# A reordered opening and other limits by stretch, in a kernel of four attention layers

## The chip, the cores and the metric

The kernel runs on one NeuronCore of one Trainium2 chip. The metric is the device time of one execution in microseconds (us), the median over runs. The engines named below are TensorE (PE, its weight loads PEld), VectorE (DVE), ScalarE (ACT), GpSimd (POOL) and the queue of SyncE (SP), which issues nearly all DMAs.

## The reference

The input `x` has 2048 tokens of 512 features, in bf16. Four layers run over it, A, B, A, B, each with a residual:

```python
x = x + _A_ref(_layernorm(x), A_wq, A_wk, A_wv, A_wo, A_beta)
x = x + _B_ref(_layernorm(x), B_wqkv, B_wo)
x = x + _A_ref(_layernorm(x), A_wq, A_wk, A_wv, A_wo, A_beta)
x = x + _B_ref(_layernorm(x), B_wqkv, B_wo)
```

Layer A cuts the tokens into 4 segments of 512. Each of 32 heads (16 wide) does causal softmax attention within the segment. Beside it stands a linear memory: with phi(t) = t + 1 for positive t and exp(t) otherwise, the sums M of phi(k) v and z of phi(k) over earlier segments give phi(q) M / (phi(q) z + 1e-6). A gate, the sigmoid of `beta` per head, mixes the two, and `wo` projects the mix. Layer B is plain attention over all 2048 tokens with 32 heads, so every query meets every key. Exponentials therefore dominate: each head of a B layer has 2048 x 2048 of them.

## The kernel before, in words

Nothing is looped on the chip. A Python planner writes one list of instructions for each engine, and semaphores follow from the reads and writes that each instruction declares. The planner estimates when each engine will be done (class Sched, `estimate`) and decides by these estimates what comes next; each engine then executes its list in order.

The attention is cut into units. One unit holds up to 3 banks of PSUM, a bank being 128 keys by 512 queries of one head. TensorE multiplies 32 rows of keys with masked queries `qm`, so that 4 heads share a row group (lines 545, 1577); ScalarE takes the exponential of the unit's banks in one instruction (line 1687) into `pT`; two units later TensorE multiplies `pT` with the values and a column of ones. The masked queries come from multiplying the queries `QA` or `QB` with a column of `par`, which is 1 for every second head's 16 features. In layer A the causal mask is either added by TensorE or applied by POOL (line 1701).

Some banks don't go through ScalarE. For them VectorE computes the exponential in integer arithmetic from PSUM: a first pass (line 1209, `dx_first`) and two adds (line 1263), into spare tiles (`dxt`, and parts of KA, QA, VA, wA, wB when these are free). A unit is then 2 banks for ScalarE and up to 2 for VectorE.

Projections, normalizations, the memory of layer A and the output projections are background tasks (Python generators). After each unit the planner runs as many of their steps as its credits and estimates allow. All thresholds of these decisions are class attributes. `PLAN` overrides some of them for a stretch of 40 units, by number; `set_limits` installs a stretch's row when its first unit comes.

The opening goes this way. SP issues the loads of the first four tiles of `x`, then the weights wk, wq, wv of layer A, `beta`, the rest of `x`, and the other weights. POOL builds the identity, the masks and constants. VectorE sums the head mask into `par` (line 667). TensorE runs `WARM` = 84 products of the identity with itself (line 651, `warm_up`), so that its clock is up. VectorE takes the statistics of the first four tiles (lines 711, 713), ScalarE their square root (719), and then loads its table for exponentials with an exponential of a constant (720). VectorE inverts (721) and normalizes the four tiles (752, into xn and oT). TensorE transposes them (580); ScalarE and VectorE copy the two halves out to `xT` (766, 767). Behind the transposes `WARM2` = 20 more products run. Then the projections of the first chunk of 128 features follow (`proj_fm`): keys, then queries, 4 products each, copied out by VectorE and ScalarE in turn (605, 603). With both the first unit can start.

Of the kernel before, what the change touches and what calls it, by code (L numbers as in the profile page):

```python
# [7 lines left out]
ALU = mybir.AluOpType  # L8
# [320 lines left out]
class Builder:  # L329
# [22 lines left out]
        20: dict(DX_LATE=900, EVAC_ACT=300, SLACK=550, PV_SKIP=500, BACK=6, CR_B=1200, R_PAIRS=2, MASK_PE=800, DIV_LATE=2500, BUSY_WAIT=500, GAP=1, BG_BANK=100, QWAIT=3, QMIN=3, HOLD_AT=40, LN1_AT=6, BUSY_BACK=800),  # L352
        21: dict(FILL_DVE=200, BACK=6, FILL=0.53, CR_W=1300, CR_B=1800, CR_A=1700, CARRY_W=0, NEARW=20, LEVEL=3, BG_BANK=400, QMIN=1, HOLD_MAX=0),
        22: dict(ACT1=200, DX_LATE=500, NEAR=10, PV_SKIP=200, EARLY=500, CR_B=1800, CARRY_W=1500, OPART=2, DX_LAG=3, MASK_PE=800, LEVEL=3, DIV_LATE=2500, DVE_LATE=800, BG_BANK=100, QUAD=0, LN1_AT=6),
        23: dict(R_LATE=1200, R_NEAR=50, FILL_DVE=200, BACK=8, CR_A=1200, NEARW=40, OPART=4, PAIRS=999, LEVEL=3, TAKEN=0.25, QUAD=0, QMIN=4, HOLD_SEGS=2),
        24: dict(R_LATE=1500, DX_LATE=900, EVAC_ACT=100, REST=12, NEAR=8, TAKEN_A=1, R_NEAR=50, PV_SKIP=100, EARLY=500, FILL_DVE=200, CR_W=1300, CR_A=1200, DX_LAG=1, LOW=20, POOL_QM=1),
        25: dict(ACT1=300, MARGIN=600, R_LATE=2200, EVAC_ACT=1500, NEAR=18, CR_W=1900, CR_B=1800, R_PAIRS=2, DX_LAG=1, PAIRS=999, DIV_LATE=800, TAKEN=0.25, DVE_LATE=800, BG_BANK=400, PHI_LATE=300),
        26: dict(MARGIN=800, REST=10, SLACK=350, EARLY=500, FILL_DVE=200, BUSY_ROOM=300, BACK=8, CR_W=1500, R_PAIRS=2, PAIRS=24, DIV_LATE=800, TAKEN=0.3, BG_BANK=100, QWAIT=8, QMIN=4, LN1_AT=6),
        27: dict(MARGIN=800, REST=4, SLACK=350, EARLY=500, FILL_DVE=200, BUSY_ROOM=300, BACK=8, CR_W=1500, PART=1, R_PAIRS=2, PAIRS=999, DIV_LATE=800, TAKEN=0.3, BG_BANK=100, QWAIT=8, QMIN=4, LN1_AT=6),
        28: dict(MARGIN=800, NEAR=5, SLACK=350, R_NEAR=10, CARRY_W=400, OPART=3, PAIRS=60, DIV_LATE=2500, TAKEN=0.3, DVE_LATE=800, BUSY_BACK=800),  # L360
        29: dict(DX_BANK=900, SLACK=700, PV_SKIP=100, EARLY=100, BUSY_ROOM=300, FILL=0.47, CR_W=1500, PART=3, R_PAIRS=2, TAKEN=0.3, DVE_LATE=800, LN1_AT=3, BUSY_BACK=800),
        30: dict(ACT1=900, MARGIN=800, REST=12, SLACK=700, PV_SKIP=100, EARLY=100, FILL=0.42, CR_W=1500, CARRY_W=400, PART=3, R_PAIRS=2, MASK_PE=800, DIV_LATE=2500, DVE_LATE=800, QWAIT=3),
        31: dict(DX_LATE=900, DX_BANK=700, REST=20, PV_SKIP=100, BUSY_ROOM=900, FILL=0.57, CR_A=1700, PART=3, R_PAIRS=2, OPART=4, MASK_PE=800, TAKEN=0.3, DVE_LATE=800, BG_BANK=100, QWAIT=3, QMIN=4),
        32: dict(MARGIN=400, DX_LATE=900, NEAR=12, PV_SKIP=100, FILL_DVE=100, BUSY_ROOM=300, FILL=0.55, CR_W=1500, R_PAIRS=2, TAKEN=0.3, GAP=3, DVE_LATE=800, QWAIT=8, QMIN=1, HOLD_AT=40),
        33: dict(MARGIN=350, DX_LATE=900, EVAC_ACT=800, NEAR=12, R_NEAR=20, PV_SKIP=100, EARLY=500, FILL=0.5, CR_W=1500, R_PAIRS=2, TAKEN=0.3, DVE_LATE=800, QWAIT=8, BUSY_BACK=800),
        34: dict(ACT1=900, R_LATE=2200, NEAR=18, BACK=2, FILL=0.55, CR_W=1500, R_PAIRS=2, DX_LAG=3, TAKEN=0.3, PE_LOW=4, GAP=3, DVE_LATE=800, QMIN=3),
        35: dict(DX_LATE=900, DX_BANK=700, REST=20, PV_SKIP=100, BUSY_ROOM=900, FILL=0.57, CR_A=1700, PART=3, R_PAIRS=2, OPART=4, MASK_PE=800, TAKEN=0.3, DVE_LATE=800, BG_BANK=400, QWAIT=3, QMIN=4),
        36: dict(ACT1=900, R_LATE=2200, REST=16, PV_SKIP=900, BUSY_ROOM=300, FILL=0.51, CR_B=1200, R_PAIRS=2, NEARW=90, OPART=4, DIV_LATE=800, DVE_LATE=800, QWAIT=8, QMIN=4, HOLD_MAX=1),
        37: dict(R_LATE=2200, DX_LATE=900, DX_BANK=900, NEAR=18, CR_W=1900, CR_B=1800, PAIRS=24, DIV_LATE=800, PE_LOW=7, DVE_LATE=800, QUAD=0),
        38: dict(REST=8, SLACK=250, R_NEAR=20, CR_W=1300, R_PAIRS=2, NEARW=90, LEVEL=1, TAKEN=0.3, LOW=20, DVE_LATE=800, QUAD=0),  # L370
# [255 lines left out]
    def setup(self):  # L626
# [24 lines left out]
        self.warm_up(self.WARM)  # L651
# [13 lines left out]
        for e_ in range(2):  # L665
            hv = hm[:, :].rearrange("p (r two) -> p two r", two=2)[:, e_, :]
            self.op("dve", (lambda e_, hv: lambda e: e.tensor_reduce(self.par[:, e_:e_ + 1], hv, axis=mybir.AxisListType.X,
                                                                     op=ALU.add))(e_, hv),
                    reads=[self.b_hm], writes=[self.b_par])
# [8 lines left out]
    def warm_up(self, n):  # L678

        al = self.new_alloc()  # L680
        for _ in range(n):
            self.mm(self.ps[:, 2560:2560 + P], self.ident[:, :], self.ident[:, :], True, True, [self.b_ident], self.banks[5], al, n=P)
# [20 lines left out]
    def ln_part(self, L, s):  # L703
# [14 lines left out]
        if (L, s) == (0, 0):  # L718
            self.op("act", lambda e: e.activation(v, var, ACT.Sqrt, bias=self.eps[:, 0:1]), reads=self.b_lnst[k] + [self.b_eps], writes=[bw], ns=230)
            self.op("act", lambda e: e.activation(self.eps[:, 1:2], self.eps[:, 0:1], ACT.Exp), reads=[self.b_eps], writes=[self.b_eps], ns=1500)  # L720
            self.op("dve", lambda e: e.reciprocal(y, v), reads=[bw], writes=[bw], ns=165)
            return k
# [22 lines left out]
    def ln_first(self, k, slot):  # L745
# [9 lines left out]
        for j in range(2):  # L755
            bank, al = self.misc(), self.new_alloc()
            base = bank.idx * 1024
            for i, (xn, bx) in enumerate(xns[2 * j:2 * j + 2]):
                for c in range(NCH):
                    o = base + c * 256 + i * 128  # L760
                    self.tr(self.psb[:, o:o + 128], xn[:, c * 128:(c + 1) * 128], [bx], bank, al)
            if j:
                self.warm_up(self.WARM2)
            src = self.psb[:, base:base + 1024].rearrange("p (c j) -> p c j", c=NCH)
            dst = self.xT[:, slot, :, j * 256:(j + 1) * 256]
            eng, fn = (("act", lambda dst, src: lambda e: e.activation(dst, src, ACT.Copy)),
                       ("dve", lambda dst, src: lambda e: e.tensor_copy(dst, src)))[j]
            self.op(eng, fn(dst, src), writes=self.b_xT[slot][2 * j:2 * j + 2], bank=bank, alloc=al, ns=(1023, 690)[j])
# [51 lines left out]
    def task_A(self, L, s):  # L820
# [1268 lines left out]
```

## Time and profile before

| | |
|---|---|
| time, median of 3 runs | 1742.31 us (1740.94 to 1742.91) |
| profiled execution, its time | 1744.39 us |
| profiled execution, its span | 1742.7 us |
| ScalarE busy | 1701.9 us (98%) |
| TensorE busy | 1627.4 us (93%) |
| VectorE busy | 1521.1 us (87%) |
| GpSimd busy | 211.6 us (12%) |
| exponentials of line 1687 | 1548 instructions, 1669.7 us |

Busy time is the time in which an engine executes instructions, without its waits. The span runs from the first to the last instruction. A row of the timeline gives start, duration, engine, line, operation, what is written and read, and in brackets the idle time ahead of it and what ended it. A row that merges several instructions lasts from the first one's start to the last one's end. A product on TensorE is pipelined: its duration covers its way through the array, and the next one starts earlier than it ends.

### The profile page before, as it was taken

The page shows a single profiled execution, that of the slowest core. Times are in us where ns is not written, and L with a number is a line of the kernel's source. Part 1 is how long each engine was busy: PE and PEld are TensorE (multiplying, and loading weights), DVE is VectorE, ACT ScalarE, POOL GpSimd, SP SyncE. Part 2 cuts the span into 40 slices and gives each one's busy share as a digit, 9 for nine tenths or more (in the row PEclk, how much of TensorE's full clock was granted, in tenths as well). Part 3 has the DMA queues.
Part 4 walks back from the last instruction along what each step waited for, and adds up shares of the span by engine and source line. Part 5 has one row for each costly group of instructions (what it writes and reads, how often), then busy time and mean ns, then how long its engine had stood idle before and what let it go on. Part 6 is the DMA issues. An engine that isn't in the chain of part 4 may idle for free.

```text
span 1742.7 us, 46922 instructions
## 1 busy us (share of the span) xinstructions
PE 1627.4 (93%) x19534; PEld 580.4 (33%) x19534; DVE 1521.1 (87%) x2937; ACT 1701.9 (98%) x1594; POOL 211.6 (12%) x325
## 2 busy tenths in 40 slices
PE   8899899999999999999999999999999999999999
PEld 5553434322222523522225222432222222222226
DVE  6757576999998699899996999989999999999997
ACT  7899999999999999999999999999999999999998
POOL 2211301110200402100003010210021000000000
PEclk9999999999999999999999999999999999999999
DMA  6110211000212131102111202011011100000000
GB/s 176 35 24 19 38 20 26 14 14 8 32 22 59 29 92 35 30 9 59 47 19 32 56 14 56 16 25 44 8 26 26 22 11 17 20 11 17 16 14 18
DMA packets 148439, 54.56 MB, mean 31 GB/s; under 512 B 128769, under 2 KB 147713, under 8 KB 148225
## 3 DMA queue, kind: packets, MB, share of 16 engines
q1 hardware_dynamic: 148224, 51.56, 13.8%
q8 instruction: 153, 2.51, 0.6%
q14 instruction: 62, 0.50, 0.1%
HBM read 18.88 MB, written 2.10 MB: 12 GB/s over the span
## 4 chain that ended last, share of the span: by engine, by line
ACT 46%; PE 30%; issue 13%; DVE 9%; DMA 1%; SPq 1%; POOL 0%; ACTq 0%; DVEq 0%; POOLq 0%
ACT pT L1687 45%; PE ps L545 30%; DVE KA L1209 1%; DVE wA L1209 1%; DVE dxt L1209 1%; DMA tb<-ub 1%; DVE wB L1209 1%; ACT amem L806 1%; SPq L612 0%; DVE lnst L711 0%; DVE qm L1577 0%; DVE dxt L1263 0%; DVE ub L1813 0%; DVE wB L1280 0%; DVE wA L1263 0%
## 5 line engine op out<-in xcount | busy, mean ns | idle before, releaser
L1687 ACT ACTIVATE pT<-ps 128x1024 bf16<-128x1024 f32 (+1 forms) x1548 | 1669.7, 1247 | 25.1 <-PE ps L545 20.2
L545 PE MATMUL ps<-qm,KB 32*128 32x512 bf16 x4096 | 561.3, 385 | 80.8 <-ACT pT L1687 65.5
L545 PE MATMUL ps<-pT,VB 128*17 128x512 bf16 x2912 | 496.2, 384 | 1.1 <-DVE wB L1209 0.3
L545 PEld LDWEIGHTS ps<-qm,KB 32*128 32x128 bf16 x4096 | 145.3, 91 | 608.7 <-ACT pT L1687 512.6
L1209 DVE TENSOR_SCALAR KA<-ps 128x512 uint16<-128x512 f32 (+1 forms) x412 | 298.1, 730 | 15.2 <-PE ps L545 11.5
L1209 DVE TENSOR_SCALAR dxt<-ps 128x512 uint16<-128x512 f32 (+1 forms) x320 | 232.1, 729 | 18.6 <-PE ps L545 15.7
L545 PE MATMUL ps<-dxt,VB 128*17 128x512 bf16 x987 | 215.9, 382 | 0.0
L545 PEld LDWEIGHTS ps<-pT,VB 128*17 128x17 bf16 x2912 | 115.8, 87 | 286.3 <-issue 273.3
L1834 POOL TENSOR_TENSOR ob<-tb,rd 128x512 bf16<-128x512 bf16 x31 | 34.5, 1114 | 806.2 <-DVE rd L1830 791.0
L545 PE MATMUL ps<-QA,VB 128*17 128x512 bf16 x423 | 124.3, 381 | 0.0
L1701 POOL TENSOR_SCALAR_AFFINE_SELECT pT<-pT 128x512 bf16<-128x512 bf16 (+4 forms) x132 | 70.1, 545 | 416.1 <-ACT pT L1687 416.1
L1209 DVE TENSOR_SCALAR wA<-ps 128x512 uint16<-128x512 f32 (+1 forms) x166 | 117.8, 716 | 2.3 <-PE ps L545 1.0
L545 PE MATMUL ps<-VA,VB 128*17 128x512 bf16 x423 | 116.8, 381 | 0.0
L545 PE MATMUL ps<-woB,zero 128*32 128x512 bf16 (+1 forms) x346 | 113.4, 383 | 0.1
L545 PE MATMUL ps<-wA,VB 128*17 128x512 bf16 x528 | 111.6, 382 | 0.0
L545 PE MATMUL ps<-qm,KA 32*128 32x128 bf16 (+2 forms) x1536 | 93.5, 256 | 18.5 <-ACT pT L1687 13.2
L545 PE MATMUL ps<-KA,VB 128*17 128x512 bf16 x423 | 107.3, 381 | 0.0
L545 PE MATMUL ps<-VA,pT 128*128 128x51 bf16 (+1 forms) x2540 | 103.9, 188 | 2.0 <-POOL pT L1701 0.9
L1577 POOL TENSOR_SCALAR qm<-QB,par 128x512 bf16<-128x512 bf16 x98 | 76.2, 788 | 232.3 <-PE ps L545 213.3
L1263 DVE TENSOR_SCALAR dxt<-dxt 128x1024 uint16<-128x1024 uint16 (+1 forms) x238 | 95.6, 425 | 1.3
L545 PEld LDWEIGHTS ps<-VA,pT 128*128 128x128 bf16 x2540 | 89.2, 97 | 20.7 <-issue 6.0
L1209 DVE TENSOR_SCALAR wB<-ps 128x512 uint16<-128x512 f32 (+1 forms) x110 | 85.1, 781 | 1.8 <-PE ps L545 0.8
(167 smaller groups left out, 1947.2 us busy)
## 6 DMA issues: line engine op xcount, KB each, us to landing
wB<-in_B_wqkv_dram SPq DMA_DIRECT2D x48, 128.0 KB, 2.4
wA<-in_A_wk_dram SPq DMA_DIRECT2D x16, 128.0 KB, 2.3
wA<-in_A_wq_dram SPq DMA_DIRECT2D x16, 128.0 KB, 2.4
wA<-in_A_wv_dram SPq DMA_DIRECT2D x16, 128.0 KB, 2.5
out_dram<-x SPq DMA_DIRECT2D x8, 256.0 KB, 2.2
x<-in_A_x_dram SPq DMA_DIRECT2D x3, 512.0 KB, 8.5
wB<-in_B_wqkv_dram SPq DMA_DIRECT2D x1, 1536.0 KB, 11.8
oT<-ob SPq DMA_TRANSPOSE x63, 2.5
```

The source lines that it names most:

```text
L545: self.sc.add("pe", lambda e: e.matmul(out, lhsT, rhs, start=start, stop=stop, skip_group_check=True), reads=reads, banks=[(bank, "w", all ...
L806: self.op("act", lambda e: e.activation(et, src, ACT.Exp), reads=bsrc, writes=self.b_amem, ns=1023, gap=915)
L1209: self.op("dve", lambda e: e.tensor_scalar(d, o, SCALE * LOG2E * 128, 127.0 * 128 + EXP_BIAS, op0=ALU.mult, op1=ALU.add), writes=[self.b_d ...
L1263: self.op("dve", (lambda d, s, c: lambda e: e.tensor_scalar(d, s, float(c), None, op0=ALU.add))(d, s, c), reads=[self.b_dxt[b][0]], writes ...
L1577: self.op(eng, (lambda m, q, col: lambda e: e.tensor_scalar(m, q, col, 0.0, op0=ALU.mult, op1=ALU.add))(m, q, col), reads=[bq, self.b_par] ...
L1687: self.sc.add("act", (lambda dst, src: lambda e: e.activation(dst, src, ACT.Exp, scale=SCALE))(dst, src), writes=self.b_pT[slot * 3 + i:sl ...
L1701: self.op("pool", (lambda blk, pat: lambda e: e.affine_select(blk, blk, pattern=pat, compare_op=ALU.is_ge, fill=0.0, base=0, channel_multi ...
L1834: self.op(eng, lambda e: e.tensor_tensor(ob, t[:, :, :, 0:16], rb, ALU.mult), reads=[br] + self.b_tb, writes=self.b_ob[oi], **(dict(ns=125 ...
```

## The change

Four things change.

- `par`, the two sums over the head mask, is no longer computed in the setup but in a new method `parity`, called behind the square root of the first statistics.
- `warm_up` takes a width. The 84 products ahead of the first transposes have 78 columns instead of 128, the 20 behind them 96.
- In the first chunk of the first segment of the first layer, queries are projected ahead of keys. The two take turns at being copied out by VectorE and ScalarE as before, so VectorE now copies the queries and ScalarE the keys.
- In `PLAN`, 18 of the rows 20 to 38 have other values (row 23 is as before). Rows 0 to 19 and 39 stay.

```diff
-        20: dict(DX_LATE=900, EVAC_ACT=300, SLACK=550, PV_SKIP=500, BACK=6, CR_B=1200, R_PAIRS=2, MASK_PE=800, DIV_LATE=2500, BUSY_WAIT=500, GAP=1, BG_BANK=100, QWAIT=3, QMIN=3, HOLD_AT=40, LN1_AT=6, BUSY_BACK=800),
+        20: dict(MARGIN=600, DX_LATE=900, EVAC_ACT=300, SLACK=550, PV_SKIP=100, CR_B=1200, R_PAIRS=2, MASK_PE=800, DIV_LATE=2500, BUSY_WAIT=500, GAP=1, BG_BANK=100, QWAIT=3, QMIN=3, HOLD_AT=40, LN1_AT=6, BUSY_BACK=800),
...
-        34: dict(ACT1=900, R_LATE=2200, NEAR=18, BACK=2, FILL=0.55, CR_W=1500, R_PAIRS=2, DX_LAG=3, TAKEN=0.3, PE_LOW=4, GAP=3, DVE_LATE=800, QMIN=3),
+        34: dict(MARGIN=350, DX_LATE=900, EVAC_ACT=800, NEAR=12, R_NEAR=20, PV_SKIP=100, EARLY=500, FILL=0.5, CR_W=1500, CARRY_W=0, R_PAIRS=2, DX_LAG=1, TAKEN=0.3, LOW=30, DVE_LATE=800, HOLD_SEGS=2, BUSY_BACK=800),
...
@@ setup
-        self.warm_up(self.WARM)
+        self.warm_up(self.WARM, 78)
...
-        for e_ in range(2):
-            hv = hm[:, :].rearrange("p (r two) -> p two r", two=2)[:, e_, :]
-            self.op("dve", (lambda e_, hv: lambda e: e.tensor_reduce(self.par[:, e_:e_ + 1], hv, axis=mybir.AxisListType.X,
-                                                                     op=ALU.add))(e_, hv),
-                    reads=[self.b_hm], writes=[self.b_par])
...
+    def parity(self):
+
+        for e_ in range(2):
+            hv = self.hmask[:, :].rearrange("p (r two) -> p two r", two=2)[:, e_, :]
+            self.op("dve", (lambda e_, hv: lambda e: e.tensor_reduce(self.par[:, e_:e_ + 1], hv, axis=mybir.AxisListType.X,
+                                                                     op=ALU.add))(e_, hv),
+                    reads=[self.b_hm], writes=[self.b_par])
+
+    def warm_up(self, n, w):
 
         al = self.new_alloc()
         for _ in range(n):
-            self.mm(self.ps[:, 2560:2560 + P], self.ident[:, :], self.ident[:, :], True, True, [self.b_ident], self.banks[5], al, n=P)
+            self.mm(self.ps[:, 2560:2560 + w], self.ident[:, :], self.ident[:, 0:w], True, True, [self.b_ident], self.banks[5], al, n=w)
...
@@ ln_part, first segment of the first layer
             self.op("act", lambda e: e.activation(self.eps[:, 1:2], self.eps[:, 0:1], ACT.Exp), reads=[self.b_eps], writes=[self.b_eps], ns=1500)
+            self.parity()
             self.op("dve", lambda e: e.reciprocal(y, v), reads=[bw], writes=[bw], ns=165)
...
@@ ln_first
-                self.warm_up(self.WARM2)
+                self.warm_up(self.WARM2, 96)
...
@@ task_A
         for c in range(NCH):
-            yield from self.proj_fm(self.wA, self.b_wA[1], 512, slot, c, self.KA[:, sl, c, :], self.b_KA[sl][c])
-            self.flags.add(("K", L, s, c))
-            yield from self.proj_fm(self.wA, self.b_wA[0], 0, slot, c, self.QA[:, sl, c, :], self.b_QA[sl][c])
-            self.flags.add(("Q", L, s, c))
+            pair = [("K", 1, self.KA, self.b_KA), ("Q", 0, self.QA, self.b_QA)]
+            for nm, i, dst, bd in pair[::-1] if (L, s, c) == (0, 0, 0) else pair:
+                yield from self.proj_fm(self.wA, self.b_wA[i], 512 * i, slot, c, dst[:, sl, c, :], bd[sl][c])
+                self.flags.add((nm, L, s, c))
```

More of the change, by code (lines that the diff above doesn't have):

```diff
@@ L355 @@
+        22: dict(ACT1=200, DX_LATE=500, NEAR=10, PV_SKIP=200, EARLY=500, FILL=0.53, CR_B=1800, CARRY_W=1500, OPART=2, DX_LAG=1, MASK_PE=800, LEVEL=3, DIV_LATE=800, DVE_LATE=800, BG_BANK=100, QUAD=0, LN1_AT=6),
         23: dict(R_LATE=1200, R_NEAR=50, FILL_DVE=200, BACK=8, CR_A=1200, NEARW=40, OPART=4, PAIRS=999, LEVEL=3, TAKEN=0.25, QUAD=0, QMIN=4, HOLD_SEGS=2),
-        24: dict(R_LATE=1500, DX_LATE=900, EVAC_ACT=100, REST=12, NEAR=8, TAKEN_A=1, R_NEAR=50, PV_SKIP=100, EARLY=500, FILL_DVE=200, CR_W=1300, CR_A=1200, DX_LAG=1, LOW=20, POOL_QM=1),
@@ L369 @@
-        37: dict(R_LATE=2200, DX_LATE=900, DX_BANK=900, NEAR=18, CR_W=1900, CR_B=1800, PAIRS=24, DIV_LATE=800, PE_LOW=7, DVE_LATE=800, QUAD=0),
-        38: dict(REST=8, SLACK=250, R_NEAR=20, CR_W=1300, R_PAIRS=2, NEARW=90, LEVEL=1, TAKEN=0.3, LOW=20, DVE_LATE=800, QUAD=0),
+        24: dict(R_LATE=1500, DX_LATE=900, EVAC_ACT=100, REST=12, NEAR=8, TAKEN_A=1, SLACK=250, R_NEAR=50, PV_SKIP=100, EARLY=500, FILL_DVE=200, CR_W=1300, CR_A=1200, DX_LAG=1, LOW=20, BG_BANK=100, POOL_QM=1),
+        25: dict(ACT1=300, MARGIN=600, R_LATE=2200, EVAC_ACT=1500, NEAR=18, CR_W=1900, CR_B=1800, R_PAIRS=2, DX_LAG=1, PAIRS=999, DIV_LATE=800, TAKEN=0.5, DVE_LATE=800, BG_BANK=400, PHI_LATE=300),
@@ L371 @@
+        38: dict(DX_LATE=700, REST=8, SLACK=250, R_NEAR=20, CR_W=1300, R_PAIRS=2, NEARW=90, PAIRS=999, LEVEL=1, LOW=20, GAP=1, DVE_LATE=800, BG_BANK=400, QUAD=0),
         39: dict(R_LATE=2200, CR_W=1900, R_PAIRS=2, PAIRS=24, DIV_LATE=800),
```

26 lines of the change are left out of this document (12 added, 14 removed).

## The prediction

> **What bounds the kernel now.** I read the page's first part, then the windows cut at every 40th exponential of line 1687 (the planner changes its limits there), then the timeline of the opening.
>
> ```profile
> PE 1627.4 (93%) x19534; PEld 580.4 (33%) x19534; DVE 1521.1 (87%) x2937; ACT 1701.9 (98%) x1594; POOL 211.6 (12%) x325
> ```
> ```profile
> 973.70:1191.60 217.90, 207.11 (x2459) 71.95 (x2458) 199.28 (x410) 216.46 (x204) 22.93 (x42) 1.00 0.15 37
> 1191.60:1705.40 513.80, 482.99 (x5028) 130.81 (x5023) 506.55 (x825) 512.88 (x522) 41.10 (x44) 1.00 0.08 16
> 1705.40:1742.70 37.30, 33.06 (x741) 22.38 (x737) 24.69 (x55) 30.12 (x32) 0.00 (x0) 0.98 0.05 17
> 14.20:82.80 68.60, 61.57 (x932) 33.26 (x932) 50.15 (x142) 60.22 (x52) 21.92 (x43) 1.00 0.31 78
> 82.80:254.40 171.60, 156.30 (x2039) 68.79 (x2039) 107.95 (x229) 163.05 (x129) 28.33 (x42) 0.97 0.16 27
> 254.40:973.70 719.30, 674.64 (x8230) 242.91 (x8222) 625.56 (x1260) 712.08 (x655) 94.44 (x140) 1.00 0.16 33
> ```
>
> The columns are stretch, length, then busy time of PE, PEld, DVE, ACT, POOL. ScalarE is the bound: of 1742.7 us it idles 40.8, and in the stretches whose limits change (20 to 38, from 973.7 us) only 1.4 + 0.9 + 7.2. There a bank of exponentials can leave ScalarE only by going to VectorE, which idles 18.6 us in the first of these windows and 7.3 in the second, which is full. The first exponential waits until 14.2 us, and what is saved ahead of it moves everything behind it:
>
> ```profile
> 1.43 7.54 PE L545 MATMUL ps<-ident 128*128 128x128 bf16 x84 [1.43 <-POOL eps L650]
> ...
> 2.75 0.35 DVE L667 TENSOR_REDUCE par<-hmask 128x1 f32<-128x4 f32 x2 [2.75 <-POOL hmask L660]
> 3.01 0.68 DVE L711 BATCH_NORM_STATS2 lnst<-x 128x6 f32<-128x512 bf16 x1
> 3.15 0.51 SPq L635 DMA_DIRECT2D wA<-in_A_wq_dram  x1
> ...
> 6.11 0.18 DVE L713 BATCH_NORM_AGGREGATE lnst<-lnst 128x2 f32<-128x6 f32 x1
> 6.33 0.30 ACT L719 ACTIVATE lnw<-lnst,eps 128x4 f32<-128x4 f32 x1 [1.73 <-DVE lnst L713]
> ...
> 6.66 0.18 DVE L721 RECIPROCAL lnw<-lnw 128x4 f32<-128x4 f32 x1 [0.37 <-ACT lnw L719]
> 6.87 0.74 DVE L752 TENSOR_SCALAR xn<-x,lnst,lnw 128x512 bf16<-128x512 bf16 x2
> 7.53 0.73 DVE L752 TENSOR_SCALAR oT<-x,lnst,lnw 128x512 bf16<-128x512 bf16 x2
> 7.94 0.20 ACT L720 ACTIVATE eps<-eps 128x1 f32<-128x1 f32 x1
> ...
> 8.81 0.61 PE L580 MATMUL ps<-ident,xn 128*128 128x128 bf16 x8
> ...
> 9.25 0.61 PE L580 MATMUL ps<-ident,oT 128*128 128x128 bf16 x8
> 9.45 1.02 ACT L766 ACTIVATE xT<-ps 128x1024 bf16<-128x1024 bf16 x1 [1.31 <-PE ps L580]
> ...
> 9.70 1.28 PE L545 MATMUL ps<-ident 128*128 128x128 bf16 x20
> 9.90 0.69 DVE L767 COPY xT<-ps 128x1024 bf16<-128x1024 bf16 x1 [1.64 <-PE ps L580]
> ...
> 10.82 1.89 PE L545 MATMUL ps<-xT,wA 128*128 128x512 bf16 x8
> ...
> 11.88 0.69 DVE L605 CAST KA<-ps 128x512 bf16<-128x512 f32 x1 [1.29 <-PE ps L545]
> 12.74 0.60 ACT L603 ACTIVATE QA<-ps 128x512 bf16<-128x512 f32 x1 [2.27 <-PE ps L545]
> 13.37 0.61 DVE L1577 TENSOR_SCALAR qm<-QA,par 128x512 bf16<-128x512 bf16 x2 [0.80 <-ACT QA L603]
> ...
> 13.78 0.39 PE L545 MATMUL ps<-qm,KA 32*128 32x512 bf16 x3 [1.08 <-DVE qm L1577]
> ...
> 14.22 2.79 ACT L1687 ACTIVATE pT<-ps 128x1536 bf16<-128x1536 f32 x2 [0.88 <-PE ps L545]
> ```
>
> Start, duration, engine and line. The first normalized tile is done at 6.87 + 0.41 = 7.28 us (two take 0.74, overlapping a little), but its transposes start at 8.81, because 84 warming products stand ahead of them on TensorE. Behind the transposes 20 more run to 10.8, while the two copies of xT end at 10.47 and 10.59. Then keys go through VectorE, queries through ScalarE, and the masked queries (1577) come last, with the product at 13.78.
>
> **The change, part by part.** The pace of a narrow product comes from these rows:
>
> ```profile
> 1.43 5.73 PE L545 MATMUL ps<-ident 128*128 128x128 bf16 x52 [1.43 <-POOL eps L650]
> ```
> ```profile
> 31.89 0.78 PE L545 MATMUL ps<-VA,pT 128*128 128x34 bf16 x24
> ```
> ```profile
> L545 PE MATMUL ps<-ident x104: 219/288/311, 1.4 to 10.8; 128*128 128x128 bf16 x104
> ```
>
> *84 products of 78 columns.* 52 products start within 5.73 - 0.31 = 5.42 us, 106 ns apart; the transposes later run (0.61 - 0.22)/7 = 56 ns apart: TensorE begins at half speed and rises near 7.1 us. Products of at most 51 columns with a full weight load each run (0.78 - 0.2)/23 = 25 ns apart, so the weight load is no floor here and 78 columns cost 78/128 of 106 = 65 ns. 84 of them end issuing at 1.43 + 5.46 = 6.9 us instead of 8.8. The bounds are 106 ns (no gain) and half of 65, if the clock rose at once; I take 65, as every early row is at half speed.
>
> *Mask sums.* Two reductions, 0.35 us together, leave the place ahead of the first statistics; those now wait for their tile:
>
> ```profile
> x<-in_A_x_dram SPq DMA_DIRECT2D x4, 128.0 KB, 2.3
> ...
> wA<-in_A_wq_dram SPq DMA_DIRECT2D x1, 512.0 KB, 5.8
> ```
> ```profile
> DMA to landing us min/median/max: 2.1/2.5/9.9
> ```
>
> Issued at 0.80, the tile lands 2.1 us later, at 2.9: the gain is 0.06 us to 0.1. The sums fit into VectorE's 0.37 us of waiting for the square root, so they cost between nothing and 0.1 us if not covered; I take nothing. Their user (1577) comes 5 us later. No DMA moves in SP's queue, and nothing moves on POOL's.
>
> *What TensorE then waits for.* Tiles 0 to 3 are normalized at 7.2, 7.55, 7.9 and 8.2; the last transpose starts at 8.43, against 9.64. ScalarE's copy cannot start before its exponential at 7.94 has ended (8.14), so it ends at 9.2 (8.14 + 0.05 + 1.02); VectorE's starts at 8.7 and ends at 9.4. The 20 products at 96 columns take 20 x 42 ns = 0.84 us from 8.48 and end at 9.3 under both copies: they no longer set the end. The first projection starts at 9.44 instead of 10.82: 1.38 us saved. Its weights are now the queries', landing at 3.15 + 5.8 = 8.95, 0.5 us ahead. That is the next limit.
>
> *Queries first.* VectorE takes queries out and masks them at once, while ScalarE takes out keys. From the start of the projection, VectorE's copy ends after 11.88 + 0.69 - 10.82 = 1.75 us, the first mask 0.35 later, ScalarE's copy after 12.74 + 0.60 - 10.82 = 2.52. The product follows that copy at 2.58 instead of 2.96: 0.38 saved. The first product comes at 12.0 instead of 13.78 and the first exponential near 12.45. The opening saves 1.75 us; if TensorE's clock rose earlier in other executions its old start would have been up to 1 us earlier, so the bounds are 0.7 and 2.2.
>
> *Limits of stretches 20 to 38.* They add no kind of instruction. They decide which banks go to VectorE, how far background work may run ahead, and who copies. The prices of a bank:
>
> ```profile
> L1209 DVE TENSOR_SCALAR KA<-ps 128x512 uint16<-128x512 f32 x205 | 138.7, 683 | 3.2 <-PE ps L545 1.5
> ...
> L1263 DVE TENSOR_SCALAR dxt<-dxt 128x1024 uint16<-128x1024 uint16 x71 | 28.9, 425 | 0.3
> ```
> ```profile
> L1687 ACT ACTIVATE pT<-ps 128x1024 bf16<-128x1024 f32 x574 | 548.5, 1132 | 1.2 <-PE ps L545 0.6
> L1687 ACT ACTIVATE pT<-ps 128x1536 bf16<-128x1536 f32 x148 | 218.8, 1520 | 1.1 <-PE ps L545 0.8
> ```
>
> A bank costs VectorE 0.68 us and half of two adds over a pair (0.425), 1.11 together. An exponential of two banks instead of three relieves ScalarE of 218.8/148 - 548.5/574 = 0.52. Filling all of the 18.6 + 7.3 us moves 23 banks, 12 us; with ScalarE's own idle 2.3 us the end is a gain of 14. The other end is a loss: one bank fewer in each of 19 stretches, 9.9. I take a third of the idle time: in the full window little can go, and in the first one layer A's banks mostly stay on ScalarE (TAKEN_A is 0 in all these rows but 24). That is 8.6/1.11 = 7.8 banks, 4.0 us. Stretches 0 to 19 keep their limits but get a new start; I take 0 for them, between a bank won and a bank lost in each, 10.4 us either way.
>
> **Sum.** The profiled execution took 1744.39 us (span 1742.7 and 1.7 around it), 2.08 above the median. 1744.39 - 1.75 - 4.0 = 1738.6, on the median's scale 1736.6.
>
> **Rivals.** *Limits bring nothing.* For it: ScalarE is busy in 512.88 of 513.80 us, VectorE in 506.55. Against it: the 18.6 us. 1742.31 - 1.75 = 1740.6.
>
> *More of VectorE is filled.* Two thirds of the idle 25.9 us: 15.5 banks, 8.1 us, 1732.5. For it speaks a price of only 1.11 us; against it, the banks of layer A, which stay.
>
> *The order slips.* The planner decides by its own clocks, which the opening shifts, while rows 0 to 19 stay. If twenty stretches each leave one more bank on ScalarE, 10.4 us are lost: 1736.6 + 10.4 = 1747.0, slower. It is even with before at (1742.31 - 1736.6)/0.52 = 11 banks and over 0.2% slower at 18. For it: VectorE idles 93.7 of 719.3 us in the long window, so places can go unused; against it: lost places can be made up there as easily.
>
> *The clock does not rise in time*, so the opening does not do what it says. Warming now ends near the moment the clock rose, and two stretches show how it falls:
>
> ```profile
> 78.70:82.10 3.40, 1.71 (x21) 1.00 0.51 102
> 82.10:85.60 3.50, 3.50 (x55) 0.51 0.37 75
> ```
>
> After a stretch with TensorE half busy, the granted clock (behind the busy time) was 0.51. If TensorE stays at half speed, the 8 projection products, 1.89 us at full speed, take up to 1.7 more, and the 20 warming ones 0.8: the opening loses 0.7 instead of gaining 1.75, 1736.6 + 2.5 = 1739.1. The Trainium skill, "TensorE: Matmul & The Clock Gate", section "Part 1: The HAM clock gate", says that the clock rises after a busy window of 3.4 us that runs free of the kernel's start. By that rule 5.5 us of warming holds a whole window in only some executions, 7.3 us in all; here the rise near 7.1 us, 5.7 after the first product, agrees with a window that began late. Its "Part 4: PE-mode transpose" adds that transposes do not count as busy, which no row here shows.
>
> **How the numbers follow.** My forecast, 1736.6 with an own range of 1734 to 1739, has 0.43; more filled 0.12; limits bring nothing 0.20; clock late 0.08; the order slips 0.17. About what a measurement can tell from no change is 0.2%, 3.5 us: faster is below 1738.8, slower above 1745.8. Nearly all of the forecast, "more filled" and a part of the clock's case are faster, 0.54; of the slipping 0.12 is over 1745.8; 0.34 remain the same. The range reaches over the other cases, 1731 to 1747.5.
>
> **What would show it.** The warming row ends issuing near 6.9; the first transpose starts near 7.3, the first projection at 9.4, products of qm and KA at 12.0, exponentials at 12.4; par's row stands between 6.2 and 6.7. From 973.7 us on, line 1209 handles some 8 banks more, and the span behind the first exponential shrinks by 4 us. I am wrong if line 1209's banks fall in the first half, if the first projection waits for wA, or if its 8 products take twice 1.89 us.

## The result and the profile after

The changed kernel takes 1737.88 us, the median of 22 runs (1734.47 to 1740.42), against 1740.56 us (1737.14 to 1743.22) for 22 runs of the kernel before beside it. The ratio is 0.9985, with a 95% interval of 0.9978 to 0.9991: 2.7 us less, 1.6 to 3.8. The sign is certain; the size, 0.15%, lies under the 0.2% that the prediction had set as the bound of "faster". Of the predicted 5.75 us about half came.

The profiled execution of after took 1740.29 us, its span is 1738.5 us; before's took 1744.39 with a span of 1742.7. Both had a mean granted clock of 0.996. All lines behind 711 have moved by 3 or 4: exponentials are now line 1691, VectorE's first pass 1213, masked queries 1581.

The first part of the page of after, and then windows cut at the same exponentials as before (the first one, the 800th and the 1000th; columns as in the prediction, behind the last engine the granted clock):

```profile
PE 1623.1 (93%) x19531; PEld 577.5 (33%) x19531; DVE 1521.2 (88%) x2928; ACT 1700.7 (98%) x1595; POOL 211.8 (12%) x321
```
```profile
12.60:970.00 957.40, 890.19 (x11187) 344.36 (x11187) 783.09 (x1631) 934.96 (x833) 144.93 (x225) 0.99 0.18 36
970.00:1186.70 216.70, 207.08 (x2463) 71.59 (x2460) 199.31 (x403) 215.07 (x203) 21.12 (x38) 1.00 0.16 38
1186.70:1738.50 551.80, 516.45 (x5757) 154.15 (x5754) 531.88 (x876) 543.65 (x553) 42.85 (x44) 1.00 0.07 16
```

The first and the last of them in before, whose middle one the prediction shows (217.90):

```profile
14.20:973.70 959.50, 892.51 (x11189) 344.95 (x11188) 783.66 (x1631) 935.36 (x833) 144.68 (x225) 0.99 0.17 35
...
1191.60:1742.70 551.10, 516.05 (x5762) 153.19 (x5756) 531.24 (x879) 542.99 (x552) 41.10 (x44) 1.00 0.07 16
```

In these two profiles the opening is shorter by 1.6 us, stretches 0 to 19 by 2.1, stretches 20 to 24 by 1.2, and the rest is longer by 0.7. Two of these four numbers are not the change's. Up to stretch 19 all engines run the same list in the same order as before, behind the opening, but for two small filling products and two instructions of VectorE that swap places near 470 us; what differs there is how often TensorE's clock fell (below). The same holds for the 0.7: after's profile has a fall at 1432 us, before's has none between 973.7 us and the last two microseconds.

The opening in the timeline of after:

```profile
1.43 4.88 PE L545 MATMUL ps<-ident 128*128 128x78 bf16 x84 [1.43 <-POOL eps L650]
...
3.03 0.69 DVE L714 BATCH_NORM_STATS2 lnst<-x 128x6 f32<-128x512 bf16 x1 [3.03 <-DMA x<-in_A_x_dram]
...
6.24 0.32 DVE L677 TENSOR_REDUCE par<-hmask 128x1 f32<-128x4 f32 x2
...
7.38 0.72 PE L580 MATMUL ps<-ident,xn 128*128 128x128 bf16 x8 [1.07 <-DVE xn L756]
...
8.58 1.01 PE L545 MATMUL ps<-ident 128*128 128x96 bf16 x20
8.78 0.69 DVE L771 COPY xT<-ps 128x1024 bf16<-128x1024 bf16 x1 [0.49 <-PE ps L580]
...
9.62 1.89 PE L545 MATMUL ps<-xT,wA 128*128 128x512 bf16 x8
...
10.68 0.69 DVE L605 CAST QA<-ps 128x512 bf16<-128x512 f32 x1 [1.21 <-PE ps L545]
...
11.54 0.60 ACT L603 ACTIVATE KA<-ps 128x512 bf16<-128x512 f32 x1 [2.38 <-PE ps L545]
...
12.19 0.39 PE L545 MATMUL ps<-qm,KA 32*128 32x512 bf16 x3 [0.69 <-ACT KA L603]
...
12.63 1.45 ACT L1691 ACTIVATE pT<-ps 128x1536 bf16<-128x1536 f32 x1 [0.49 <-PE ps L545]
```

The chain is the predicted one: transposes wait for normalized tiles and no longer for warming products, and the first product of queries and keys waits for ScalarE's copy of the keys. It starts at 12.19 (predicted 12.0), the first exponential at 12.63 (12.45).

### The profile page after: what moved, and what is told of

It reads as the page before. It is cut to its first block, busy times and chain, and to the rows that moved or that the text cites. A ratio compares the mean times of both kernels' runs of the same rounds, so it can differ in the third digit from the quotient of the medians.

```text
span 1738.5 us, 46910 instructions
## 1 busy us (share of the span) xinstructions
PE 1623.1 (93%) x19531; PEld 577.5 (33%) x19531; DVE 1521.2 (88%) x2928; ACT 1700.7 (98%) x1595; POOL 211.8 (12%) x321
## 4 chain that ended last, share of the span: by engine, by line
ACT 48%; PE 31%; issue 13%; DVE 7%; SPq 0%; POOL 0%; DMA 0%; ACTq 0%; DVEq 0%
ACT pT L1691 47%; PE ps L545 31%; DVE KA L1213 1%; DVE dxt L1213 1%; ACT amem L810 1%; DVE lnst L714 1%; SPq L612 0%; DVE wA L1213 0%; PE ps L560 0%; POOL xn L743 0%; DVE VA L605 0%; DVE qm L1581 0%; DVE dxt L1267 0%; DVE dxt L1284 0%; DVE VB L605 0%
## 5 line engine op out<-in xcount | busy, mean ns | idle before, releaser
L545 PE MATMUL ps<-QA,VB 128*17 128x512 bf16 x420 | 118.3, 384 | 0.0
L1705 POOL TENSOR_SCALAR_AFFINE_SELECT pT<-pT 128x256 bf16<-128x256 bf16 (+4 forms) x128 | 67.6, 541 | 413.8 <-ACT pT L1691 413.8
L545 PE MATMUL ps<-woB,zero 128*32 128x512 bf16 (+1 forms) x353 | 117.5, 382 | 0.1
L545 PE MATMUL ps<-KA,VB 128*17 128x512 bf16 x420 | 101.0, 383 | 0.0
L1267 DVE TENSOR_SCALAR dxt<-dxt 128x1024 uint16<-128x1024 uint16 (+1 forms) x216 | 85.7, 420 | 1.2
```

Source lines behind the costliest of these rows:

```text
L545: self.sc.add("pe", lambda e: e.matmul(out, lhsT, rhs, start=start, stop=stop, skip_group_check=True), reads=reads, banks=[(bank, "w", all ...
L1267: self.op("dve", (lambda d, s, c: lambda e: e.tensor_scalar(d, s, float(c), None, op0=ALU.add))(d, s, c), reads=[self.b_dxt[b][0]], writes ...
L1705: self.op("pool", (lambda blk, pat: lambda e: e.affine_select(blk, blk, pattern=pat, compare_op=ALU.is_ge, fill=0.0, base=0, channel_multi ...
```

## The experiments

### One half of the change alone

`opening_only` is after with the old rows 20 to 38, `limits_only` is before with the new rows. In both, the lists of instructions agree with those of before or after wherever the text of the kernel does, but for two or three small filling products and one swapped pair on VectorE, so the two halves can be added.

Of `opening_only`, against after (rows 20 to 38 in the same way):

```diff
-        21: dict(FILL_DVE=200, BACK=10, FILL=0.53, CR_W=1300, CR_B=1800, CR_A=1700, CARRY_W=0, NEARW=20, LEVEL=3, BG_BANK=400, QMIN=1, HOLD_MAX=0),
+        21: dict(FILL_DVE=200, BACK=6, FILL=0.53, CR_W=1300, CR_B=1800, CR_A=1700, CARRY_W=0, NEARW=20, LEVEL=3, BG_BANK=400, QMIN=1, HOLD_MAX=0),
```

Of `limits_only`, against after:

```diff
-        self.warm_up(self.WARM, 78)
+        self.warm_up(self.WARM)
...
-            self.parity()
...
-                self.warm_up(self.WARM2, 96)
+                self.warm_up(self.WARM2)
...
-            pair = [("K", 1, self.KA, self.b_KA), ("Q", 0, self.QA, self.b_QA)]
-            for nm, i, dst, bd in pair[::-1] if (L, s, c) == (0, 0, 0) else pair:
```

> The new opening with all the old limits; the orders of all engines are then those of before behind the opening, except for three small filling products. Theory A (the two halves add: opening 1.6 us by the first exponential's start, 12.63 against 14.22 us, limits 1.1 us, the rest of the measured 2.7): first exponential near 12.6, time 1.6 us under before, 0.9991. Theory B (the opening is all of it): 2.7 us under before, 0.9985. Theory C (the limits are all of it and the opening's saving is lost again before the end): within 0.5 us of before.

> The old opening with the new limits of stretches 20 to 38. Theory A: first exponential near 14.2, the same times up to stretch 20, then 0.5 to 2 us less; in all 1.1 us under before, 0.9994. Theory B: no difference beyond 0.5 us. Theory C: 2.7 us under before. A fourth, that the limits fit only behind the new opening: slower than before.

Measured: `opening_only` 1737.9 us (1736.52 to 1741.15, 12 runs), ratio 0.9986 (0.9978 to 0.9995); `limits_only` 1737.7 us (1735.43 to 1741.11, 12 runs), ratio 0.9987 (0.9979 to 0.9995). Each half alone is about as fast as both together, which the sum of two independent gains doesn't allow.

The clock resolves it: TensorE's granted clock falls to half now and then within the kernel, and some executions have more of these falls than others. The mean granted clock of a run and its time go together: after's 22 runs have means of 1740.3 at 0.996, 1739.4 at 0.997, 1737.3 at 0.998 and 1736.1 at 0.999; before's of 1742.6 at 0.997, 1740.7 at 0.998, 1739.8 at 0.999 and 1737.7 at 1.000. A line with one slope and a constant for each kernel, through the 143 runs of the nine kernels timed in rounds, gives 1.47 us (plus or minus 0.10) for each 0.001 of clock, with 0.57 us left over. Read at clock 1.000, before stands at 1738.1, `opening_only` at 1736.6, `limits_only` at 1736.2 and after at 1734.6, each within 0.4.

So the opening is worth 1.5 us, the limits 1.9, and together 3.5: they add. The medians mix in that after's runs had a slightly lower mean clock (0.9978 over 22, against 0.9982 over 55 of before's), about 0.7 us. Whether the change itself makes falls more frequent is not shown: `opening_only` had a mean of 0.9989 and `limits_only` of 0.9987, and the clocks of the 22 runs of before that stand beside after are not on record.

Windows of the two profiles, cut at the same exponentials. `opening_only`, in which the clock never fell until the last two microseconds:

```profile
12.50:965.80 953.30, 880.17 (x11124) 342.69 (x11185) 782.90 (x1631) 934.68 (x833) 145.33 (x225) 1.00 0.18 36
965.80:1183.70 217.90, 206.70 (x2452) 71.97 (x2459) 199.29 (x410) 216.43 (x203) 22.98 (x42) 1.00 0.15 37
1183.70:1734.80 551.10, 516.05 (x5760) 153.29 (x5757) 531.49 (x879) 543.15 (x552) 41.17 (x44) 1.00 0.08 16
```

`limits_only`:

```profile
968.10:1184.90 216.80, 206.79 (x2456) 71.66 (x2460) 199.43 (x403) 215.15 (x203) 21.13 (x38) 1.00 0.16 37
1184.90:1735.30 550.40, 514.92 (x5755) 154.13 (x5754) 531.93 (x876) 543.59 (x553) 42.85 (x44) 1.00 0.07 16
```

The old rows give 217.90 and 551.10 in before and in `opening_only`, the new ones 216.70 to 216.80, and 550.40 where the clock doesn't fall: 1.1 and 0.7 us, 1.8 in all. The sum is firm, the split less so, since the new rows share out the banks among units in another way. At the 1000th exponential they have issued 3924 products with masked queries against 3926 of the old ones; at 0.30 us each (217.90 us for 716 of them, an estimate) about half of the 1.1 us is work that comes behind the cut. Stretches 0 to 19 take 953.30 without a fall, 959.50 in before with four windows at half clock, 957.40 in after with three: 1.4 to 1.6 us for a window.

What the limits moved is seen in ScalarE's exponentials from stretch 20 on, and in its last copies of transposed tiles, first before, then after:

```profile
L1687 ACT ACTIVATE pT<-ps 128x1024 bf16<-128x1024 f32 x595 | 568.4, 1129 | 1.4 <-PE ps L545 0.6 <-ACT pT L1687 0.2
L1687 ACT ACTIVATE pT<-ps 128x1536 bf16<-128x1536 f32 x154 | 227.1, 1520 | 1.1 <-PE ps L545 0.8
...
L1099 ACT ACTIVATE oT<-ps 128x256 bf16<-128x256 bf16 x1 | 0.4, 384 | 3.3 <-PE ps L580 3.3
```
```profile
L1691 ACT ACTIVATE pT<-ps 128x1024 bf16<-128x1024 f32 x601 | 574.1, 1122 | 2.0 <-PE ps L545 1.4
L1691 ACT ACTIVATE pT<-ps 128x1536 bf16<-128x1536 f32 x149 | 220.8, 1534 | 1.7 <-PE ps L545 1.1
...
L1103 ACT ACTIVATE oT<-ps 128x256 bf16<-128x256 bf16 x1 | 0.4, 384 | 2.4 <-PE ps L580 2.4
```

595 x 2 + 154 x 3 = 1652 banks before, 601 x 2 + 149 x 3 = 1649 after. Three banks left ScalarE. At 0.52 us each that would be 1.6 of the 1.8 us, but the windows say otherwise. From stretch 20 on ScalarE is busy 759.6 us in `opening_only` and 758.7 in `limits_only`, 0.8 or 0.9 less, and it idles 9.4 and 8.5 us, 0.9 or 1.0 less. So about half of the gain is idle time, and nearly all of that stands at the very end: behind the last exponentials the new rows leave TensorE less to do, and ScalarE waits 2.4 us instead of 3.3 for its last transposed tile.

### A part of the new rows

If each row were better by itself, either half of the rows would bring a part of the 1.9 us.

`limits_20_24` keeps the new rows 20 to 24 and has the old rows 25 to 38, of which this is the first, against after:

```diff
-        25: dict(ACT1=300, MARGIN=600, R_LATE=2200, EVAC_ACT=1500, NEAR=18, CR_W=1900, CR_B=1800, R_PAIRS=2, DX_LAG=1, PAIRS=999, DIV_LATE=800, TAKEN=0.5, DVE_LATE=800, BG_BANK=400, PHI_LATE=300),
+        25: dict(ACT1=300, MARGIN=600, R_LATE=2200, EVAC_ACT=1500, NEAR=18, CR_W=1900, CR_B=1800, R_PAIRS=2, DX_LAG=1, PAIRS=999, DIV_LATE=800, TAKEN=0.25, DVE_LATE=800, BG_BANK=400, PHI_LATE=300),
```

`limits_25_38` is the counterpart, with the old rows 20 to 24, among them the row 21 shown above.

> After, but rows 25 to 38 are the old ones. My prediction's term put most of the limits' gain here, where VectorE had idled 18.6 us: 3 us under the opening alone. The two profiles say that this window went from 217.9 to 216.7 us, 1.2 less: then 2.8 us under before, as fast as after or faster. A rival: the old rows 25 to 38 meet another state and lose it again, 1.6 us under before or less.

> After, but rows 20 to 24 are the old ones. Going by the two profiles the later rows bring nothing (551.1 against 551.8 us, and 550.3 without a clock drop that only after had): 1.6 to 2.4 us under before. If the later rows carry the gain of the limits: 2.7 us under before or more. If they need the state that the new rows 20 to 24 leave: less than 1.6.

Measured: 1743.78 us (1741.24 to 1746.04, 11 runs), ratio 1.0019 (1.0011 to 1.0028), and 1744.86 us (1742.74 to 1747.81, 8 runs), ratio 1.0026 (1.0016 to 1.0036). Both are slower than before, and slower than after by 6 to 7 us. On the line above, at clock 1.000, they stand at 1741.2 and 1743.4, 6.6 and 8.8 us over after. The rival expected for both, a gain under 1.6 us, had the direction and not the size. Their windows from stretch 25 on, in the same order:

```profile
1185.50:1742.50 557.00, 520.46 (x5755) 155.15 (x5756) 533.29 (x880) 546.00 (x555) 45.73 (x44) 1.00 0.07 16
```
```profile
1183.30:1741.00 557.70, 523.41 (x5746) 157.77 (x5745) 534.03 (x878) 546.17 (x557) 43.91 (x44) 1.00 0.07 16
```

557.00 and 557.70 stand against 551.10 (old rows throughout) and 550.40 (new ones throughout). ScalarE is busy 2.3 to 3.2 us more than in after or before, with 3636 and 3637 banks in the whole kernel against 3635 of before and 3632 of after, and it idles 11.0 and 11.5 us of the window where the unbroken sets leave 8.1 and 6.8. The window of rows 20 to 24 is as short in `limits_20_24` as with all the new rows (216.80). So a row fits the state that the rows ahead of it leave, and in both splits the old rows behind the new ones, or the new ones behind the old, lose more than the whole change gains. This is the mechanism of the rival "the order slips", with a price of some 6 to 9 us, though the change itself doesn't set it off.

### The parts of the opening

Each part alone, on before.

`narrow_only`:

```diff
-        self.warm_up(self.WARM)
+        self.warm_up(self.WARM, 78)
...
-                self.warm_up(self.WARM2)
+                self.warm_up(self.WARM2, 96)
```

`queries_only`:

```diff
-            yield from self.proj_fm(self.wA, self.b_wA[1], 512, slot, c, self.KA[:, sl, c, :], self.b_KA[sl][c])
...
+            for nm, i, dst, bd in pair[::-1] if (L, s, c) == (0, 0, 0) else pair:
```

`parity_only`, which also takes the two sums out of the setup:

```diff
+            self.parity()
```

> Before, with only the narrower warming products (78 and 96 columns). My theory: the first projection starts near 9.6 us as in after, keys first, so the first product of qm and KA comes 2.96 us behind it, near 12.6, and the first exponential near 13.0. Rival (the sums over the mask had to move too, or queries to come first, for the narrow products to pay): projection no earlier than 10.5.

> Before, with only the queries ahead of the keys in the first chunk. My theory: first product of qm and KA 2.58 us behind the start of the first projection instead of 2.96; the projection itself starts where the 128-column warming lets it, between 9.8 and 11.4 by the moment at which TensorE's clock rises. Rival: 2.96 as before, because the masks wait for something else.

> Before, with only the sums over the mask moved behind the square root. My theory: worth nothing; first statistics within 0.1 us of 3.01, end of the four statistics within 0.1 us, reciprocal still right behind the square root. Rival: 0.3 us earlier, the duration of the two sums.

Single runs took 1739.05, 1738.22 and 1740.11 us, all under before's median and within its range, so the timelines say more. `narrow_only`:

```profile
1.43 5.64 PE L545 MATMUL ps<-ident 128*128 128x78 bf16 x84 [1.43 <-POOL eps L650]
...
9.59 1.89 PE L545 MATMUL ps<-xT,wA 128*128 128x512 bf16 x8
12.55 0.39 PE L545 MATMUL ps<-qm,KA 32*128 32x512 bf16 x3 [1.08 <-DVE qm L1577]
```

`queries_only`:

```profile
9.67 1.89 PE L545 MATMUL ps<-xT,wA 128*128 128x512 bf16 x8
...
12.25 0.39 PE L545 MATMUL ps<-qm,KA 32*128 32x512 bf16 x3 [0.69 <-ACT KA L603]
```

`parity_only`:

```profile
10.26 1.89 PE L545 MATMUL ps<-xT,wA 128*128 128x512 bf16 x8
...
13.23 0.39 PE L545 MATMUL ps<-qm,KA 32*128 32x512 bf16 x3 [1.08 <-DVE qm L1581]
```

Queries first shortens the way from the projection to the product of queries and keys from 2.96 or 2.97 us (12.55 - 9.59, 13.23 - 10.26) to 2.58 (12.25 - 9.67): 0.38, as worked out. The start of the projection depends on when the clock rose. With 128 columns it came at 10.82 in before (rise at 7.09 us), 10.26 in `parity_only` (5.92) and 9.67 in `queries_only` (4.58). With 78 columns it came at 9.59 in `narrow_only` (7.09) and at 9.62 in after (5.29). The moments of the rise are from the traces' record of the granted clock. The narrow products are worth 1.2 us where the clock rises late and next to nothing where it rises early; what they give is a start that hardly depends on it any more. Moving the mask sums brought nothing: `parity_only` starts its statistics at 3.04, before at 3.01, since the first tile hasn't landed earlier.

### Nearly no warming

In after, the warming products have 24 columns. They stay 104 in number, so TensorE's list stays in order.

```diff
-            self.mm(self.ps[:, 2560:2560 + w], self.ident[:, :], self.ident[:, 0:w], True, True, [self.b_ident], self.banks[5], al, n=w)
+            self.mm(self.ps[:, 2560:2560 + 24], self.ident[:, :], self.ident[:, 0:24], True, True, [self.b_ident], self.banks[5], al, n=w)
```

> After, with warming products of 24 columns in both places (the planner still counts 78 and 96, so that the order stays). They end near 3.8 us. My rival 'the clock does not rise in time': the first projection runs at half speed, its 8 products take up to 3.6 instead of 1.89 us, the first exponential comes 1 to 2.5 us later than the 12.63 of after, and half speed lasts into the first units. If warming is not what raises the clock: 12.6 again.

The run took 1737.96 us with a mean clock of 0.999; after's runs at that clock have a mean of 1736.1. The timeline:

```profile
10.00 3.28 PE L545 MATMUL ps<-xT,wA 128*128 128x512 bf16 x8 [0.35 <-DVE xT L771]
...
13.97 0.39 PE L545 MATMUL ps<-qm,KA 32*128 32x512 bf16 x3 [0.69 <-ACT KA L603]
```

The clock rose at 12.85 us, and the eight products took 3.28 instead of 1.89. The product of queries and keys came 1.8 us later than in after. This is the price of the rival "the clock does not rise in time", which the prediction had put at 2.5; with 78 and 96 columns it wasn't paid in any profile (rise at 4.58 to 7.28 us in all with full warming).

### The falls of the clock

The runs of one kernel spread over 6 us, more than the change is worth. A fall in after, with the stretch ahead of it, and the same stretch 31 in after (with the fall) and in `limits_only` (without; the same instructions):

```profile
1428.60:1432.10 3.50, 2.59 (x24) 0.99 0.00 0
1432.10:1435.50 3.40, 3.40 (x27) 0.50 0.19 39
```
```profile
1421.60:1461.60 40.00, 37.85 (x365) 9.41 (x360) 38.42 (x61) 38.49 (x42) 2.40 (x3) 0.96 0.04 8
```
```profile
1419.90:1458.40 38.50, 36.36 (x365) 9.30 (x358) 38.27 (x61) 38.34 (x42) 2.40 (x3) 1.00 0.04 8
```

One window of 3.4 us at half clock costs 1.5 us of a kernel that ScalarE bounds, since ScalarE runs dry behind TensorE: it idles 1.5 of 40.00 us, against 0.2 of 38.50. The falls in the profiles, those of the last microseconds left aside, stand at few places: 80 to 82, 192 to 195, 461, 1410 and 1432 us. Ahead of the first, TensorE waits for masked queries, ahead of the second for a transposed tile from a DMA (timeline of after):

```profile
80.31 0.58 PE L545 MATMUL ps<-qm,KA 32*128 32x512 bf16 x3 [1.39 <-DVE qm L1581]
...
193.88 1.86 PE L545 MATMUL ps<-xT,wB 128*128 128x512 bf16 x4 [2.26 <-DMA xT<-xn]
```

The product at 193.88 takes twice its time; the clock had fallen at 193.02, before that wait was over. The theory: a wait of 1.4 to 2.3 us lets the clock fall if it fills enough of a window that the chip counts by itself, so that one execution is caught and another not. The record of the clock supports the window: in every profile the falls and rises lie whole multiples of 3.413 us behind the first rise (in before the rise at 7.09, the falls at 82.18, 194.82 and 461.06, which are 22, 55 and 133 windows later). `filled_lulls` is after with products of zeros in five such waits, into banks where they change nothing; `filled_level` fills the first two only, and takes 16 products out of the opening's warming (68 of 96 columns for 84 of 78), so that later products keep their place in TensorE's list; `filled_four` adds two more places to that.

```diff
+    LULLS = {1046: 6, 2473: 10, 5409: 2, 6521: 2, 16094: 1}
...
+            for _ in range(self.LULLS[at]):
+                o, z, w = self.ps[0:cols or 128, col0:col0 + 512], self.zero[:, 0:cols or 128], self.woB[:, 0, :]
+                new = Op("pe", 0, (lambda o, z, w, st: lambda e: e.matmul(o, z, w, start=st, stop=st, skip_group_check=True))(o, z, w, not cols), "lull")
...
+                ops.insert(at, new)
```

`filled_level`, against `filled_lulls` (`pe_no` keeps the planner's own count of TensorE's instructions where it was):

```diff
-        self.warm_up(self.WARM, 78)
+        self.warm_up(self.WARM - 16, 96)
+        sc.pe_no[-1] += 2 * 16
-    LULLS = {1046: 6, 2473: 10, 5409: 2, 6521: 2, 16094: 1}
+    LULLS = {1046 - 16: 6, 2473 - 16: 10}
```

`filled_four`, against `filled_level`:

```diff
-    LULLS = {1046 - 16: 6, 2473 - 16: 10}
+    LULLS = {1046 - 16: 6, 2473 - 16: 10, 5409 - 16: 2, 16094 - 16: 1}
```

> After, with 21 products of zeros put into five places of TensorE's list where it waits (6 near 79 us, 10 near 191, 2 near 455, 2 near 570, 1 near 1428); all else in the same order. Theory (the runs of one kernel differ by how many windows of 3.4 us run at half clock, 1.5 us each, and those come where TensorE streams under 0.3 of a window): granted clock 0.999 to 1.0 in nearly all runs, none of the drops near 80 and 193 us, median 1.5 to 3 us under after, 1735 to 1736.5, ratio to before 0.997 to 0.998. Rival (the clock is only a sign of something else, or added products cost what they save): the same time as after, 0.9985, or slower by up to 1 us at equal clock.

> After, with 6 products of zeros near 79 us and 10 near 191, and 16 fewer warming products in the opening (68 of 96 columns, as many columns in all as 84 of 78), so that every later instruction of TensorE keeps its number in the list. Theory (the fill itself costs nothing; the 1.15 us that stretch 21 lost in the filled kernel came with the shift of TensorE's instructions by 21): stretch 21 takes 40.4 us again, span near 1733, median 1735 to 1736, 1 us under the filled kernel. Rival (the loss in stretch 21 has another cause): 41.5 us again, the median of the filled kernel, 1736.7.

> The same with 2 more products near 455 us and 1 near 1428. Theory: the last two places at which a window may fall under 0.3 are covered, nearly all runs at a clock of 1.0, 0.2 to 0.5 us under the kernel with two places in the median, unless the shift by 2 and 3 instructions behind 455 us brings a loss like that of stretch 21.

| kernel | median us (range, runs) | ratio to before (95%) | runs by granted clock |
|---|---|---|---|
| after | 1737.88 (1734.47 to 1740.42, 22) | 0.9985 (0.9978 to 0.9991) | 0.996: 4, 0.997: 5, 0.998: 5, 0.999: 8 |
| filled_lulls | 1736.68 (1736.08 to 1737.59, 11) | 0.9978 (0.9969 to 0.9987) | 0.999: 1, 1.000: 10 |
| filled_level | 1735.38 (1734.75 to 1736.70, 6) | 0.9970 (0.9959 to 0.9982) | 0.998: 1, 0.999: 2, 1.000: 3 |
| filled_four | 1735.11 (1734.64 to 1736.80, 6) | 0.9968 (0.9956 to 0.9980) | 0.999: 1, 1.000: 5 |

The spread goes from 6 us to 2, over fewer runs, and nearly all runs keep the clock. With their TensorE instructions in place, or within 2 or 3 of it, the last two beat both kernels: 5.2 to 5.5 us under before, 2.5 to 2.8 under after. On the line above `filled_level` stands at 1734.6 at clock 1.000, as after does, so its whole gain over after is the clock. In the profile of `filled_level` the zero products stand where TensorE waited, and the product behind them takes its ordinary time:

```profile
190.08 2.32 PE L2060 MATMUL ps<-woB,zero 128*128 128x512 bf16 x10
192.42 1.02 PE L545 MATMUL ps<-xT,wB 128*128 128x512 bf16 x4
```

That the falls near 80 and 193 us go with these waits is thus shown; those at 461, 1410 and 1432 us stand behind shorter ones (0.53 us is the longest in the window ahead of 1432.06). What exactly the chip counts is not shown. It isn't busy time as the profile counts it: in `limits_25_38` the windows that end at 80.99 and 193.63 us had TensorE busy for 1.56 and 1.50 of 3.41 us and no fall followed, while in after the one that ends at 1432.06 had 2.50 and one did.

An estimate from the traces comes nearer. Count the time in which columns stream (0.216 us for 512, from the ten products above), overlaps once and products of 32 rows at a third, in windows laid 0.1 us behind the grid of the falls: the 13 windows ahead of a fall then hold at most 0.31 of their length, and none of the some 6500 others in the 13 profiles less than 0.32. The weights were chosen afterwards to fit, so no run tests this count.

`filled_lulls` has another cost: at clock 1.000 it stands at 1736.7, after at 1734.6. In its stretch 21, far from any filled wait, ScalarE idles 1.05 us, and the stretch takes 41.6 us instead of 40.4:

```profile
1005.50:1047.10 41.60, 39.13 (x361) 10.71 (x363) 39.30 (x83) 40.55 (x42) 3.09 (x4) 1.00 0.21 51
```
```profile
1005.30:1045.70 40.40, 38.24 (x361) 10.44 (x363) 39.01 (x83) 40.35 (x42) 3.23 (x4) 1.00 0.21 53
```

The first row is `filled_lulls`, the second `filled_level`: the same instructions, with 20 products more ahead of them on TensorE than in after in the one, and as many as in after in the other. `filled_four`, with 2 more, takes 40.4 as well. So the loss goes with the place in TensorE's list. The trace shows the next link: VectorE waits for a small transpose by DMA (`tb`), first in `filled_lulls`, then in `filled_level`:

```profile
1034.12 0.35 DVE L1837 RECIPROCAL rd<-tb 128x32 f32<-128x32 bf16 x1 [1.29 <-DMA tb<-ub]
```
```profile
1032.50 0.35 DVE L1838 RECIPROCAL rd<-tb 128x32 f32<-128x32 bf16 x1
```

It took 3.9 us from issue to landing in the one and 2.4 in the other, and VectorE's first passes and ScalarE's exponentials behind it came late. In `filled_lulls` a load of instructions, 16 KB on DMA queue 8, started at 1032.00 us, while the transpose was under way; in `filled_level` the same load started at 1034.23, behind it. That this load held the transpose up fits the place in the list, but no run tests it, and it stays open.

## Why the prediction was right, and where it was not

*The opening: 1.75 us predicted, 1.6 in the two profiles, 1.5 at equal clock.* Warming products of 78 columns at 65 ns held to 0.1 us where the clock rose at the same time as in before (`narrow_only`: 5.64 us from the first start to the last end, against 5.46 of issuing). Transposes started at 7.34 to 7.38 (7.3). The projection came at 9.6 and not at 9.44, though, as predicted, the 20 products of 96 columns did not set the end: the last of them started at 9.39 (their row ends at 9.59, and one takes 0.21). TensorE waited for VectorE's copy, which was done at 9.47 instead of 9.4, and the first product came 0.15 us behind it, where the prediction had allowed 0.04. The same 0.15 stands in `little_warming` (copy done at 9.85, product at 10.00). Weights of the queries were not waited for. Queries first gave 0.38 to the digit. An early rise of the clock, which gave the lower bound of 0.7, is real, and the bound was not low enough: the first projection behind the old warming moved between 9.67 and 10.82, and from 9.67 the new opening gains 0.05 + 0.38 = 0.4.

*The mask sums* cost nothing, as taken, in VectorE's wait for the square root (6.24, 0.32). The small gain of an earlier start, 0.06 to 0.1, didn't come: the first tile lands at 3.03.

*Rows 0 to 19: 0 predicted, 0 measured.* The order didn't slip: the difference of 2.1 us in the two profiles goes with one window more at half clock in before.

*The limits: 4.0 us predicted, 1.9 measured at equal clock.* The step that failed is "I take a third of the idle time". 3 banks moved and not 7.8. The price of 0.52 did not hold either: ScalarE's busy time fell by 0.8 or 0.9 for the three, and the other half of the gain, the shorter wait at the end, is in no term of the prediction. In stretches 20 to 24 VectorE's idle time fell from 18.6 us to 17.4 only, and behind them it stayed at 19.9 (551.10 - 531.24, 551.80 - 531.88). Nothing in the trace had pointed to a third; the truth lay half way between the forecast and the rival that the limits bring nothing. That rival's time, 1740.6, was on the scale of the three runs shown, and before's median fell from 1742.31 to 1740.56 with more runs.

*The sum.* 3.5 us less at equal clock stand against 5.75 predicted, and 2.7 in the medians. The predicted 1736.6 lies 1.3 under the measured 1737.9, within its own range, and that is partly luck: the gain was put 3.1 us too high, and the three runs of before that it was taken from stood 1.75 above the longer median, which hides more than half of the error. The chance of 0.54 for "faster by over 0.2%" leaned on the 4.0; the measured class has the 0.34.

*What the prediction had not seen* is the clock inside the kernel. It quoted a fall at 82 us, as evidence on the opening, and didn't ask how often such falls come or what one costs: four windows in that profile, 6 us.

The Trainium skill, "TensorE: Matmul & The Clock Gate", section "Part 1: The HAM clock gate", has a free-running window of about 3.4 us, after which the clock rises if it was busy and falls if it was idle. The length agrees (3.4 us from 1432.10 to 1435.50), and a free-running window agrees with a rise that moved from 4.58 to 7.28 us over the profiles. Idle is too strict here: in the stretch ahead of 1432.10, TensorE was busy, as the profile counts it, in 2.59 of 3.50 us.

## What to carry to other kernels

Before a gain of a tenth of a per cent is judged, compare runs at the same granted clock, or fill the waits of TensorE that let it fall: here this was worth 2.5 us, nearly as much as the change, and it took away two thirds of the spread. Work at the head of this kernel was a gain that lasted to its end, since everything waits for it, and its size could be read off the timeline, once it was known when the clock rose. Limits of a planner belong to the state that the rows ahead of them leave: here the set could be taken or left as a whole only, and the idle time of an engine was no measure of what the new set filled.

## What the chip showed that was not expected

- Waits of TensorE of 1.39 and 2.26 us, shorter than the window of 3.41 us, were enough in some executions for a fall of the granted clock to 0.50 for 3.4 us, and for twice that at 193 us; each window costs 1.5 us.
- The clock rose between 4.58 and 7.28 us in executions with full warming, 3.2 to 5.9 us after the first product.
- With 20 products more ahead of it in TensorE's list, a stretch of the same instructions took 1.2 us longer; with their number made up for elsewhere, it took its old time. A transpose by DMA landed after 3.9 us instead of 2.4, beside a load of instructions of 16 KB; that the load held it up is not shown.
